# Column order of the one-pass matrix products in a fused Mamba-2 scan and low-rank mixer

## The chip, the cores and the metric

The kernel runs on one core of one Trainium2 chip. The metric is the device time of one execution in microseconds, from runs without the profiler; one more execution was recorded by the hardware profiler, and all times inside the kernel come from that one. Engines are named as the profile names them: PE is TensorE with PEld its weight loads, DVE is VectorE, ACT is ScalarE, POOL is GpSimd, SP is SyncE with its DMA queue SPq.

## The reference

A Mamba-2 scan over 4 batches, 8 heads, 768 positions, in chunks of 32, gives `x` of shape (4, 768, 256). A mixer follows, and its last two products are where this change lies:

```python
xt = x.transpose(0, 2, 1)
h = xt @ U @ V                            # U 768 x 32, V 32 x 768
u = x + h.transpose(0, 2, 1)
ch = np.maximum(u @ w_ch1, 0.0) @ w_ch2   # 256 -> 1024 -> 256
return (u + ch).astype(np.float32)
```

## The kernel before

**Layout.** The mixer works on `u` turned over: its 256 channels lie on the partitions (two halves, `NCB` = 2) and the tokens along the free dimension. The 768 tokens of a batch are cut into three blocks of 256 (`HS`). So there are twelve blocks, and a product is always 128 x 128 weights against 256 columns, one column for each token. `w_ch1` gives 1024 hidden channels, eight groups of 128 (`m`), of which a step takes two. The result of a step is a PSUM tile of 128 x 2 x 256, one bank; the banks carry the tags `x` and `z` (three each, by turns) and `w` (two).

**Two kinds of products.** The first two blocks of batch 0 are multiplied in full precision (`plain`, and the second branch of `down`): each such product shows as two MATMUL records. The other ten blocks use the type fp32r, of which a product shows as one record, a one-pass product. To keep precision, each fp32r operand is split into three tensors: a near part (`v` = 0), a far part (`v` = 1) and a combination of both (`v` = 2). The products of `v` = 0 and 1 are added up in PSUM, ACT scales the sum in place (`scaled`, L858), and the products of `v` = 2 are added on top.

**The steps.** For block `j` and step `i`, `first` (letter `f` in the plan) makes the products of `v` = 0 and 1, eight of them, and the scaling. `second` (`e`) adds the four of `v` = 2 and has ACT write the ReLU. `third` (`h`) makes the far and the combined tensors of the hidden channels on DVE. `down` (`d`) multiplies the hidden channels with `w_ch2`: for each `v`, each half `n` of the output channels and each half of the hidden groups a call of `products` with four of them, 48 in a block; after the last, DVE adds `u` and the block goes out. The very last block of batch 3 goes through `rows` instead, which has the hidden channels as weights and `w_ch2` as the 256 columns.

**How many.** Ten blocks have 16 products in `first` for each of `v` = 0 and 1, and 16 in `second`: 480. Nine blocks go through the one-pass branch of `down`, with 16 for each `v`: 432. `rows` has 48. That makes 960 one-pass products.

**What sets the order.** Nothing is scheduled by a tool: the long strings in `PLANS` name every step in the order in which it is written, and each engine runs its instructions in that order. The steps of the scan for batches 1 to 3 (`gram` L591, `inter` L721, `intra` L746, `state` L626) stand between the mixer's steps of earlier batches. From about 161 us on the scan is over and PE has products of the mixer alone.

**All products pass one line.** `nc.tensor.matmul` in `products` (L853) issues them all; its tiles tell them apart: `x<-u,w` and `z<-u,w` are `first` and `second`, `x<-words,w` and `z<-words,w` are `down`, `x<-w,words` and `z<-w,words` are `rows`, and those with `yT,w1f` or `words,o` the full-precision ones. Operands are dense: the 256 columns of `rhs` and of the PSUM half lie side by side in a partition. A few products elsewhere are not dense: `keep` (L394, L397) writes PSUM in groups of 8 columns with gaps of 8 between them, and `gram` (L591) reads its 128 columns alternately from two places that lie 128 elements apart.

Of the kernel before, what the change touches and what calls it, by code (L numbers as in the profile page):

```python
# [74 lines left out]
def kernel(  # L75
# [27 lines left out]
    nc = tc.nc  # L103
# [46 lines left out]
    def bank(tag, *dims):  # L150
        t = psum.tile([P, *dims], FP32, tag=tag, name=tag, bufs=BANKS[tag])
        if any(fills):
            flat = t if len(dims) == 1 else t.rearrange(
                {2: "p a b -> p (a b)", 3: "p a b c -> p (a b c)"}[len(dims)])
            small(flat, fills[1])
            idle(flat, fills[0])
        fills[:] = 0, 0
        return t
# [7 lines left out]
    class Kept:  # L166
# [23 lines left out]
        out=a_sb,  # L190
# [4 lines left out]
    pairs = [(b, q) for b in range(NB) for q in range(NPR)]  # L195
# [122 lines left out]
    for v in range(2):  # L318
        half = slice(v * H, v * H + H)
# [15 lines left out]
    for g in range(2):  # L335
# [3 lines left out]
        out=la.rearrange("p b c h -> p b h c"),  # L339
# [19 lines left out]
    for v in range(2):  # L359
        half = slice(v * H, v * H + H)  # L360
# [110 lines left out]
    def prep(k, c=0, n=2):  # L471

        b, q = pairs[k]
        if "BC" not in st.setdefault(k, {}):
            st[k]["BC"] = att.tile([P, 2, 2, NH, N], FP32, tag="BC", name="BC")
        for g in [slice(4) if n == 2 else slice(c, c + 1) if c < 2 else slice(2, 4)]:
            part = st[k]["BC"].rearrange("p i c h n -> p (i c) h n")[:, g]
            vector.tensor_tensor(
                out=part, in0=bc_sb[k].rearrange("p h i c n -> p (i c) h n")[:, g],
                in1=F[:, b, q].rearrange("p h i c -> p (i c) h")[:, g, :, None].to_broadcast(  # L480
                    part.shape), op=ALU.mult)
# [316 lines left out]
    def mixer(b):  # L798
# [35 lines left out]
        def block(j):  # L834
            return uT[:, :, ts(j, HS)]
# [12 lines left out]
            vector.tensor_tensor(out=far, in0=u, in1=near.bitcast(FP32), op=ALU.subtract)  # L848
            joined(near, far, both)

        def products(t, pairs, start):
            for lhsT, rhs in pairs:
                nc.tensor.matmul(out=t, lhsT=lhsT, rhs=rhs, start=start, stop=True,  # L853
                                 skip_group_check=True)
                start = False

        def scaled(t):
            nc.scalar.activation(t, t, AF.Copy, scale=1.0 + EPS)  # L858

        def words(dtype):  # L860
            t = raw.tile([P, 2 * WCOLS], INT32, tag="words", name="words", bufs=NWORDS)
            return t.bitcast(dtype).rearrange("p (v m t) -> p v m t", v=2, m=2)

        def plain(j, i):

            if i % 2 == 0:
                gT[j, i // 2] = words(FP32)
            t = bank("xz"[i % 2], 2, HS)
            for m in range(2):
                products(t[:, m], [(w1f[i][:, n, ts(m, P)], block(j)[:, n]) for n in range(NCB)],  # L870
                         m == 0)
            nc.scalar.activation(gT[j, i // 2][:, i % 2], t, AF.Relu)

        def terms(j, m, which):
            return [(w1[v][:, n, ts(m, P)], us[j][v][:, n]) for v in which for n in range(NCB)]

        def first(j, i):

            gs["t", j, i] = t = bank("xz"[i % 2], 2, HS)
            for m in range(2):  # L880
                products(t[:, m], terms(j, 2 * i + m, (0, 1)), m == 0)
            scaled(t)

        def second(j, i):

            t = gs["t", j, i]
            for m in range(2):
                products(t[:, m], terms(j, 2 * i + m, (2,)), False)
            if i % 2 == 0:
                gs["both", j, i // 2] = words(FP32R)  # L890
            nf = words(FP32R)
            gs[j, i] = [nf[:, 0], nf[:, 1], gs["both", j, i // 2][:, i % 2]]
            nc.scalar.activation(gs[j, i][0], t, AF.Relu, scale=NEAR)  # L893
# [43 lines left out]
        def down(j):  # L937

            def terms(n, which, half):
                return [(w2[v][:, m, ts(n, P)], gs[j, m // 2][v][:, m % 2])  # L940
                        for v in which for m in range(NQ * half, NQ * half + NQ)]

            def added_to(t, n=slice(None), sl=slice(None)):
                u = block(j)[:, n, sl]
                vector.tensor_tensor(out=u, in0=t[:, n, sl], in1=u, op=ALU.add)

            t = bank("xz"[j % 2], NCB, HS)
            if b or j >= PLAIN:
                for v in range(3):
                    for n in range(NCB):  # L950
                        for half in range(2):
                            products(t[:, n], terms(n, (v,), half), v + n + half == 0)
                            if v == 1 and n and half:
                                scaled(t)
                            if v == 2 and n and half:
                                added_to(t)
                            yield
            else:
                for n in range(NCB):
                    for half in range(2):  # L960
                        products(t[:, n], [(w2f[m // 2][:, m % 2, ts(n, P)],
                                            gT[j, m // 4][:, m // 2 % 2, m % 2])
                                           for m in range(NQ * half, NQ * half + NQ)],
                                 n + half == 0)
                        if n and half:
                            added_to(t)
                        yield
            if b or j == NBL - 1:
                o = mix.tile([P, 2 * WCOLS], FP32, tag="o", name="o") if b else raw.tile(
                    [P, 2 * WCOLS], FP32, tag="words", name="words", bufs=NWORDS)  # L970
                o = o[:, :NCB * HS].rearrange("p (n i) -> p n i", n=NCB)
                vector.transpose(out=o, in_=block(j))
                for r in range(4):
                    nc.sync.dma_start(
                        out=out[b, ts(j, HS)].rearrange(
                            "(k t) (n a c) -> a t n k c", t=Q, n=NCB, c=Q)[r],
                        in_=o[ts(r, Q)].rearrange("p n (k c) -> p n k c", c=Q))
                yield
                return
            o = raw.tile([P, 2 * WCOLS], FP32, tag="words", name="words", bufs=NWORDS)  # L980
            o = o[:, :HS // P * DM].rearrange("p (k n d) -> p k n d", k=HS // P, n=NCB)
            t = bank("w", HS // P, NCB, P)
            for n in range(NCB):
                for k in range(HS // P):
                    nc.tensor.transpose(out=t[:, k, n], in_=block(j)[:, n, ts(k, P)],
                                        identity=ident)
            nc.scalar.copy(out=o, in_=t)
            nc.sync.dma_start(
                out=out[b].rearrange("(j k p) m -> j p k m", j=NBL, p=P)[j],
                in_=o.rearrange("p k n d -> p k (n d)"))  # L990
            yield
# [4 lines left out]
        def piece(j):  # L996
            next(downs.setdefault(j, (rows if b >= ROWS and j == NBL - 1 else down)(j)))

        return SimpleNamespace(p=project, x=mixed, a=added, S=split, f=first, e=second, h=third,
                               d=piece, U=plain)  # L1000

# [10 lines left out]
    def spread():  # L1012

        nc.scalar.copy(out=UU, in_=U_sb[:, :, None].to_broadcast([P, NC, 2, RK]))

        v = [bank(t, VS // 2) for t in "xz"]
        for q in range(4):
            for i in range(2):
                nc.tensor.matmul(out=v[i][ts(q, Q)],
                                 lhsT=ident.rearrange("p (r q) -> p q r", q=4)[:, 2 * (q % 2) + i],  # L1020
                                 rhs=Vq, start=True, stop=True, skip_group_check=True)
        for i in range(2):
            nc.scalar.copy(out=V4[:, ts(i, VS // 2)], in_=v[i])
# [32 lines left out]
    def ytokens_of(k, v):  # L1056
# [6 lines left out]
                 j=crossed, y=yout, t=sided, L=load, Q=lambda k, c: prep(k, c, 1),  # L1063
# [4 lines left out]
                 v=lambda n: spread())  # L1068
# [54 lines left out]
```

## Time and profile before

| | us |
|---|---|
| three runs | 214.03, 215.01, 215.75 |
| median | 215.01 |
| span of the profiled execution, first to last instruction | 216.2 |
| last MATMUL starts in the profiled execution | 212.8 |

The profiled execution has no time of its own beside its span. The span is 1.2 us above the median of the runs and 0.4 us above the longest. A sum made from its rows is therefore used as a difference, and put on the median. "Busy" of PE joins overlapping matmuls; the pace of a row of products is better read from start to start, which the timeline gives: a row there is a run of equal instructions with the start of the first, the time to the end of the last, and their count.

### The profile page before, as it was taken

The numbers are of one execution on the slowest core, as the hardware profiler recorded it, in microseconds if no ns is written. First come the engines' busy times: TensorE is split into PE (matmuls) and PEld (weight loads), VectorE is DVE, ScalarE is ACT, GpSimd is POOL, SyncE is SP. The second block draws the span as 40 slices with busy tenths as digits, with TensorE's granted clock in tenths as the row PEclk, the third lists the DMA queues.
The fourth block names the chain that finished last, engine by engine and source line by source line (L and its number), as shares of the span: only waits on it lengthen the run. The fifth ranks groups of instructions, "written<-read, shape, count | busy, mean of one in ns | idle before, by whom it ended". The sixth has DMA issues, their size and how long they took to land.

```text
span 216.2 us, 7556 instructions
## 1 busy us (share of the span) xinstructions
PE 205.8 (95%) x3214; PEld 183.6 (85%) x3214; DVE 173.4 (80%) x363; ACT 121.0 (56%) x279; POOL 6.3 (3%) x22
## 2 busy tenths in 40 slices
PE   7988987999999999999999999899999999999994
PEld 4766755787889997998999998589998999999993
DVE  4498869988999999999899986759966398759841
ACT  3454646659968857186488451668612675444310
POOL 4121000000000000000000000000000000000000
PEclk9999997999999999999999999999999999999999
DMA  6998677996553379447666846544600000323344
GB/s 89 123 117 197 76 186 170 218 247 149 77 71 52 65 195 124 110 60 102 92 103 108 190 91 150 80 74 100 137 12 0 0 5 0 52 38 64 48 97 97
DMA packets 120177, 21.43 MB, mean 99 GB/s; under 512 B 110096, under 2 KB 118352, under 8 KB 120144
## 3 DMA queue, kind: packets, MB, share of 16 engines
q1 hardware_dynamic: 120144, 20.95, 53.3%
q8 instruction: 25, 0.41, 0.9%
q14 instruction: 8, 0.07, 0.1%
HBM read 14.39 MB, written 6.55 MB: 97 GB/s over the span
## 4 chain that ended last, share of the span: by engine, by line
PE 62%; DVE 22%; SPq 5%; ACT 4%; issue 3%; DMA 2%; POOL 0%; DVEq 0%; POOLq 0%; ACTq 0%
PE x L853 28%; PE z L853 21%; DVE words L177 7%; SPq L203 5%; DVE S L177 3%; DMA words<-in_moe_w_ch_dram 2%; DVE yT L177 2%; DVE w L177 2%; DVE M L177 2%; DVE BC L177 1%; PE x L139 1%; PE w L626 1%; PE x L591 1%; DVE u L177 1%; PE z L746 1%
## 5 line engine op out<-in xcount | busy, mean ns | idle before, releaser
L177 DVE SCALAR_TENSOR_TENSOR words<-words 128x512 fp32r<-128x512 f32 (+6 forms) x60 | 39.3, 668 | 2.6 <-ACT words L429 0.5
L853 PE MATMUL x<-words,w 128*128 128x256 f32 x288 | 38.5, 281 | 0.1
L853 PEld LDWEIGHTS x<-words,w 128*128 128x128 f32 x288 | 35.3, 189 | 1.8 <-issue 1.2
L853 PE MATMUL x<-u,w 128*128 128x256 f32 x240 | 34.6, 283 | 0.0
L853 PE MATMUL z<-u,w 128*128 128x256 f32 x240 | 33.0, 279 | 0.0
L858 ACT ACTIVATE x<-x 128x512 f32<-128x512 f32 (+1 forms) x27 | 15.5, 577 | 29.6 <-PE x L853 27.5
L853 PEld LDWEIGHTS x<-u,w 128*128 128x128 f32 x240 | 30.5, 188 | 0.6 <-ACT yT L766 0.3
L853 PEld LDWEIGHTS z<-u,w 128*128 128x128 f32 x240 | 30.0, 188 | 0.1
L858 ACT ACTIVATE z<-z 128x512 f32<-128x512 f32 (+1 forms) x24 | 13.6, 572 | 12.7 <-PE z L853 12.7
L853 PE MATMUL z<-words,w 128*128 128x256 f32 x144 | 19.9, 282 | 0.0
L853 PEld LDWEIGHTS z<-words,w 128*128 128x128 f32 x144 | 18.1, 189 | 0.9 <-issue 0.9
L177 DVE SCALAR_TENSOR_TENSOR words<-x,words 128x512 fp32r<-128x512 f32 x20 | 13.7, 683 | 5.4 <-ACT words L893 5.4
L177 DVE SCALAR_TENSOR_TENSOR words<-z,words 128x512 fp32r<-128x512 f32 x20 | 13.6, 682 | 2.3 <-ACT words L893 2.2
L893 ACT ACTIVATE words<-x 128x512 fp32r<-128x512 f32 x20 | 12.0, 598 | 3.6 <-PE x L853 3.6
L591 PE MATMUL x<-Cm,T 32*64 32x128 f32 x192 | 12.1, 310 | 1.6 <-DVE yT L177 1.2
L177 DVE TENSOR_TENSOR yT<-x,yT 128x384 f32<-128x384 f32 (+1 forms) x15 | 9.2, 614 | 5.5 <-PE x L853 2.7
L177 DVE SCALAR_TENSOR_TENSOR S<-S,kept,w 128x64 f32<-128x64 f32 x40 | 11.2, 279 | 2.3 <-PE w L626 0.6
L893 ACT ACTIVATE words<-z 128x512 fp32r<-128x512 f32 x20 | 11.8, 598 | 1.9 <-PE x L853 1.3
L658 ACT ACTIVATE Sm<-S,slot 128x128 f32<-128x128 f32 (+1 forms) x18 | 6.0, 386 | 9.9 <-DVE S L177 9.9
L591 PEld LDWEIGHTS x<-Cm,T 32*64 32x64 f32 x192 | 7.5, 131 | 4.1 <-DVE yT L177 1.5
L177 DVE TENSOR_TENSOR BC<-bc,F 128x512 f32<-128x512 f32 (+2 forms) x18 | 8.8, 517 | 2.6 <-ACT F L379 1.3
L591 PE MATMUL z<-Cm,T 32*64 32x128 f32 x192 | 10.5, 311 | 0.0
(154 smaller groups left out, 368.5 us busy)
## 6 DMA issues: line engine op xcount, KB each, us to landing
words<-in_moe_w_ch_dram SPq DMA_DIRECT2D x7, 512.0 KB, 5.3
squares<-w1f SPq DMA_DIRECT2D x52, 64.0 KB, 1.9
x<-in_x_dram SPq DMA_DIRECT2D x24, 128.0 KB, 4.0
out_dram<-o SPq DMA_DIRECT2D x32, 64.0 KB, 2.2
bc<-in_B_dram SPq DMA_DIRECT2D x24, 64.0 KB, 3.5
bc<-in_C_dram SPq DMA_DIRECT2D x12, 128.0 KB, 3.8
T<-squares SPq DMA_DIRECT2D x6, 256.0 KB, 3.9
ytok<-squares SPq DMA_DIRECT2D x6, 256.0 KB, 3.1
```

Source lines behind the costliest of these rows:

```text
L139: nc.tensor.matmul(out=t[:, :m * w].rearrange("p (m i) -> p m i", i=w), lhsT=ident, rhs=ident[:, None, :w].to_broadcast([P, m, w]), start= ...
L177: self.last = call(*args, **kwargs)
L203: op = nc.sync.dma_start(**kwargs)
L591: nc.tensor.matmul(out=g[r][cols, c], lhsT=s["T"][rows, 0, c, cols], rhs=s["Cm"][rows, :, :, ts(2 * c + p, Q)].rearrange("r v t i -> r v i ...
L626: nc.tensor.matmul(out=s["A"][p][ts(r, Q), v], lhsT=s["bd"][half, v, 2 * r:2 * r + 2].rearrange("p h n -> p (h n)"), rhs=x_sb[k][half, v, ...
L658: nc.scalar.activation(s["Sm"][:, sl, v], s["S"][:, sl, ts(v, D)], AF.Copy, scale=slot[:, v, None])
L746: product = nc.tensor.matmul(out=y[n][p][ts(v, Q), c], lhsT=x_sb[k][half, c, h], rhs=s["M"][half, h // 2, c, h % 2], start=fresh(k, n, p, ...
L853: nc.tensor.matmul(out=t, lhsT=lhsT, rhs=rhs, start=start, stop=True, skip_group_check=True)
L858: nc.scalar.activation(t, t, AF.Copy, scale=1.0 + EPS)
L893: nc.scalar.activation(gs[j, i][0], t, AF.Relu, scale=NEAR)
```

## The change

`products` takes a width. Where one is given, the 256 columns of the PSUM half and of `rhs` are both walked in another sequence: they are cut into groups of `width` columns, the even groups are taken first and the odd ones after them. Each column still meets its own column of the result, so the sums are the same. The first products of a sum (`v` = 0), the full-precision ones and those of `rows` keep the plain order; `first` takes 64 for `v` = 1, `second` takes 16, and `down` takes 32 for `v` = 1 and 4 for `v` = 2.

```diff
+        def columns(t, width):
+
+            return t.rearrange("p (a b c) -> p b a c", b=2, c=width) if width else t
+
-        def products(t, pairs, start):
+        def products(t, pairs, start, width=None):
             for lhsT, rhs in pairs:
-                nc.tensor.matmul(out=t, lhsT=lhsT, rhs=rhs, start=start, stop=True,
-                                 skip_group_check=True)
+                nc.tensor.matmul(out=columns(t, width), lhsT=lhsT, rhs=columns(rhs, width), start=start,
+                                 stop=True, skip_group_check=True)
                 start = False
...
-                products(t[:, m], terms(j, 2 * i + m, (0, 1)), m == 0)
+                products(t[:, m], terms(j, 2 * i + m, (0,)), m == 0)
+                products(t[:, m], terms(j, 2 * i + m, (1,)), False, 64)
             scaled(t)
...
-                products(t[:, m], terms(j, 2 * i + m, (2,)), False)
+                products(t[:, m], terms(j, 2 * i + m, (2,)), False, 16)
...
-                            products(t[:, n], terms(n, (v,), half), v + n + half == 0)
+                            products(t[:, n], terms(n, (v,), half), v + n + half == 0,
+                                     (None, 32, 4)[v])
```

No instruction moves: on every engine the same ones stand in the same order with the same waits, and only the shape of the columns differs. On PE near the end of the kernel before, where the `e` step of one block and `down` of another alternate (`u_3087` is the combined tensor of a block of `u`, `w_79` that of `w_ch1`; `w_82` and `w_83` are the far and the combined tensors of `w_ch2`):

```order
L853 MATMUL x<-words,w_82 128x256 x4
L853 MATMUL z<-u_3085,w_77 128x256 x2
L853 MATMUL z<-u_3086,w_78 128x256 x2
L853 MATMUL x<-u_3087,w_79 128x256 x4
L853 MATMUL x<-words,w_83 128x256 x12
```

The same place now:

```order
L857 MATMUL x<-words,w_82 128x2x4x32 x4
L857 MATMUL z<-u_3085,w_77 128x256 x2
L857 MATMUL z<-u_3086,w_78 128x2x2x64 x2
L857 MATMUL x<-u_3087,w_79 128x2x8x16 x4
L857 MATMUL x<-words,w_83 128x2x32x4 x12
```

The last number of a shape is the width of a group, the one before it how many groups of one kind there are, and the 2 ahead of it stands for even and odd.

## The prediction

> **What bounds the kernel now.** I read the page first: how busy each engine is, the clock granted to PE, the chain that ended last, and the groups of L853.
>
> ```profile
> PE 205.8 (95%) x3214; PEld 183.6 (85%) x3214; DVE 173.4 (80%) x363; ACT 121.0 (56%) x279; POOL 6.3 (3%) x22
> PEclk9999997999999999999999999999999999999999
> PE 62%; DVE 22%; SPq 5%; ACT 4%; issue 3%; DMA 2%; POOL 0%; DVEq 0%; POOLq 0%; ACTq 0%
> L853 PE MATMUL x<-words,w 128*128 128x256 f32 x288 | 38.5, 281 | 0.1
> L853 PE MATMUL x<-u,w 128*128 128x256 f32 x240 | 34.6, 283 | 0.0
> L853 PE MATMUL z<-u,w 128*128 128x256 f32 x240 | 33.0, 279 | 0.0
> L853 PE MATMUL z<-words,w 128*128 128x256 f32 x144 | 19.9, 282 | 0.0
> ```
>
> The reader sees PE busy for 95% of the span, most of the chain on PE, and 912 one-pass products with 0.1 us of idle time ahead of them in all. Next I took the stages, with the time of each engine in a stretch, the granted clock and the DMA share.
>
> ```profile
> 69.00:100.00 31.00, 30.84 (x467) 27.63 (x474) 30.13 (x61) 20.22 (x45) 0.00 (x0) 1.00 0.58 106
> 100.00:127.00 27.00, 27.00 (x512) 25.71 (x506) 25.22 (x49) 16.95 (x42) 0.00 (x0) 1.00 0.66 119
> 127.00:161.00 34.00, 33.30 (x610) 30.22 (x610) 26.59 (x54) 18.21 (x46) 0.00 (x0) 1.00 0.48 94
> 161.00:213.00 52.00, 52.00 (x444) 51.03 (x440) 34.96 (x55) 22.47 (x42) 0.00 (x0) 1.00 0.21 35
> ```
>
> Columns: length, PE, PEld, DVE, ACT, POOL, clock, DMA share, GB/s. The one-pass products begin in the first of these stretches. From there on the clock is 1.00, and the last 52 us are PE from end to end, while DVE has a third of them free. So a nanosecond on a product there is a nanosecond on the kernel; before 161 us nearly so, since PE lacks only 0.9 us of 92 in the first three rows.
>
> What sets the pace of a product? Its mean duration (281) overlaps its neighbours; the pace is read from start to start in the timeline.
>
> ```profile
> 73.34 0.60 PE L985 MATMUL w<-ident,yT 128*128 128x128 f32 x4
> 73.78 3.62 PE L853 MATMUL z<-words,o 128*128 128x256 f32 x16
> ...
> 119.82 1.52 PE L853 MATMUL x<-words,w 128*128 128x256 f32 x12
> 121.18 0.62 PE L853 MATMUL z<-words,w 128*128 128x256 f32 x4
> ...
> 168.16 2.05 PE L853 MATMUL z<-u,w 128*128 128x256 f32 x16
> 170.05 0.64 PE L853 MATMUL x<-u,w 128*128 128x256 f32 x4
> ```
>
> Twelve one-pass products take 121.18 - 119.82 = 1.36 us, 113 ns each; sixteen later take 170.05 - 168.16 = 1.89 us, 118 ns each. Both paces hold for long stretches and don't go with a tile. Two neighbours are quicker for the same work. A full-precision record of 256 columns goes over them twice: with the 379 ns of one record taken off the 3.62 us, (3.62 - 0.38) / 15 = 216 ns, or 108 ns for 256 column steps. A transpose, which also loads 128 x 128 weights, goes at (0.60 - 0.27) / 3 = 110 ns, with one duration of 272 ns taken off; the rows of these two durations:
>
> ```profile
> L853 PE MATMUL z<-words,o 128*128 128x256 f32 x32 | 7.4, 379 | 0.0
> L985 PE MATMUL w<-ident,yT 128*128 128x128 f32 x8 | 1.2, 272 | 0.0
> ```
>
> So a one-pass product has 108 ns of columns, and 5 to 10 ns more from elsewhere. In that pair of operations a weight load of 128 columns stands against each 256 columns, and the last stage's row has PEld busy for 51.03 of 52 us. [...] Then columns may become 5 to 10 ns slower before anyone sees it.
>
> **The change part by part.** It adds no instruction, no wait and no transfer, and its order on each engine is unchanged; SP's and POOL's queues aren't touched. Of the 960 one-pass products 608 walk their columns in groups: 160 in groups of 64 (`first`), 160 of 16 (`second`), 144 of 32 and 144 of 4 (`down`). Of the 144 of width 4, five blocks' worth, 80, stand in the last 52 us. The only unknown is what a jump between groups costs, on the side of PSUM and on the side of the columns read.
>
> On the PSUM side the trace has a pair: `keep` writes 192 dense columns at L387, and 192 in groups of 8 with gaps of 8 at L394.
>
> ```profile
> 7.89 0.49 PE L387 MATMUL z<-la,after 128*128 128x192 f32 x2
> 8.22 0.43 PE L389 MATMUL z<-la,onward 128*128 128x160 f32 x2
> 8.49 0.49 PE L394 MATMUL z<-la,middle 128*128 128x192 f32 x2
> 8.82 0.43 PE L397 MATMUL z<-la,high 128*128 128x160 f32 x2
> 9.09 0.43 PE L397 MATMUL z<-la,low 128*128 128x160 f32 x2
> ```
>
> L387 takes 8.22 - 7.89 = 0.33 us and L394 8.82 - 8.49 = 0.33 us: gaps in PSUM cost nothing there. They are full-precision products, which go over their columns twice; whether one pass is as forgiving, no row shows. [...]
>
> On the reading side the nearest row is `gram`, whose neighbouring columns lie 128 elements apart, so that every column is a jump.
>
> ```profile
> 125.92 0.30 PE L591 MATMUL x<-Cm,T 32*64 32x128 f32 x2
> 125.93 0.30 PE L591 MATMUL z<-Cm,T 32*64 32x128 f32 x2
> 125.95 0.30 PE L591 MATMUL x<-Cm,T 32*64 32x128 f32 x2
> 125.96 0.30 PE L591 MATMUL z<-Cm,T 32*64 32x128 f32 x2
> 126.06 0.30 PE L591 MATMUL x<-Cm,T 32*64 32x128 f32 x2
> ...
> 126.20 0.30 PE L591 MATMUL x<-Cm,T 32*64 32x128 f32 x2
> ```
>
> Eight records, side by side on different parts of the array, start every 126.20 - 126.06 = 0.14 us. Each goes twice over 128 columns, 256 column steps: 140 ns against 108 for dense ones. Part of the 32 ns may be the array's four row strips and not the jumps. So the price for 256 scattered steps is 0 to 32 ns if each pass pays alone, and up to 64 if one pass has to fetch as many columns as two did there.
>
> Width 4 has 64 groups in 256 columns. I take the scattered price for it, 140 ns, as the nearest row that I have, though fewer jumps may cost less. In the last 52 us that is 80 x (140 - 118) = 1.8 us; for the other 64, at paces of 113 and 118, 64 x (140 - 115.5) = 1.6 us. Widths 16, 32 and 64 have 16, 8 and 4 groups. At the same price for a jump they add 32 x 16/64 = 8 ns, 4 and 2 to the 108, which ends at 116 or below: within 3 ns of the load's cover, at most 160 x 3 = 0.5 us at the pace of 113 and nothing at 118, so nothing is taken. If that cover is gone, by loads at the transposes' 110, they cost 160 x 6 + 144 x 2 = 1.2 us. DVE and ACT get later products and wait; in the last stage DVE's 35 of 52 us leave room. The sum is +3.4 us. Bounds for width 4 are 0 and 144 x (172 - 116) = 8.1 us.
>
> The profiled execution ran 216.2, 1.2 above the median 215.0; the difference goes on the median: 215.0 + 3.4 = 218.4.
>
> **The rivals.**
>
> *Nothing is seen.* Groups of 4 are as good as dense, or slower by less than the load covers. For it speak L394 and the 5 to 10 ns of cover. The time is 215.0, give or take what the two paces make: should the last stage fall to 113 ns, 440 x 5 = 2.2 us are gained, and the earlier stretches at 118 would lose as much. Chance 0.26.
>
> *Faster.* The 5 to 10 ns above 108 need not be the load's own: they may be the column reads and the weight reads getting in each other's way, with two ways of falling into step (113 and 118). Columns in another sequence would then break the step. At the transposes' 110, the 272 changed products of the last stage gain 8 ns each and the 336 before it about 5.5: 2.2 + 1.8 = 4.0 us, 211.0; the pace of 113 in the last stage alone would give 212.8. I name 212.0. For it: a transpose loads equally many weights and is 3 to 8 ns quicker. Against it: each pace holds through many tiles at different places. [...] Chance 0.22.
>
> *Much slower.* [...] Chance 0.07 and 0.05.
>
> **How the numbers follow.** The forecast, width 4 at the scattered price, has the rest: 0.40, with its own range 216.5 to 223. About 1%, 2.2 us, is what a measurement of this kernel can tell from no change. Faster by more than that: 0.21 of the faster rival and 0.03 of a lucky pace, 0.24. Within it: 0.22 of the rival without effect, 0.05 of a small price for width 4, 0.01 of a weak gain, 0.28. Slower: 0.35 of the forecast, 0.12 of the much slower rival and 0.01 of an unlucky pace, 0.48. The range runs from 211.0, the faster rival's full gain, to 223.0, the upper bound of width 4: beyond it lie 0.12 above and some 0.06 below.
>
> **What would show it.** In the changed kernel's timeline of the last stage, `down` with `w_83` (width 4) should go at about 140 ns from start to start, the rest at 113 to 118 as before, and PE should stay without gaps up to the last product, which starts some 3 us later. Width 4 at 118 or less shows the first rival; widths 64 to 4 at 110 or below the second; any width at 200 or above the third. The forecast is wrong if width 4 isn't the slowest of the four, or if plain-order products change their pace too: then the cause lies in the loads and not in the columns.

## The result, and the profile after

| | before | after |
|---|---|---|
| median of 13 runs each, us | 214.13 | 216.71 |
| lowest and highest | 213.32, 216.94 | 215.94, 220.88 |
| span of the profiled execution | 216.2 | 215.0 |

The changed kernel is slower: ratio 1.0125, 95% interval 1.0098 to 1.0153, which on 214.13 is 2.7 us (2.1 to 3.3). The ratio leaves out runs more than 1.5% above the fastest of their kernel, such as the one of 220.88. The profiled execution after took 216.69, at its median; so 1.7 us lie around its span. With as much around its span of 216.2, that of before took some 217.9, an estimate that is above each of its 13 runs, and its clock row has a slice of 7 that the other has not. The two spans can't be set against each other, but the stretch of one-pass products can, with care. It runs from the start of the first to that of the last: 69.5 to 212.8 before, 67.1 to 211.5 after, 143.3 and 144.4 us.

The page of the changed kernel, with the rows that answer to those of before:

```profile
PE 205.9 (96%) x3214; PEld 183.7 (85%) x3214; DVE 173.4 (81%) x363; ACT 121.0 (56%) x279; POOL 6.3 (3%) x22
...
PEclk9999999999999999999999999999999999999999
...
PE 82%; DVE 6%; SPq 4%; ACT 2%; DMA 2%; issue 2%; POOL 0%; DVEq 0%; POOLq 0%; ACTq 0%
...
L857 PE MATMUL x<-words,w 128*128 128x256 f32 x288 | 38.9, 282 | 0.1
...
L857 PE MATMUL x<-u,w 128*128 128x256 f32 x240 | 34.9, 285 | 0.0
L857 PE MATMUL z<-u,w 128*128 128x256 f32 x240 | 33.4, 281 | 0.0
...
L857 PE MATMUL z<-words,w 128*128 128x256 f32 x144 | 20.1, 283 | 0.0
```

Each group of products has grown by 0.2 to 0.4 us, and nothing else has appeared: no new wait, the same counts. Where it sits shows in the timeline near the end, where the kernel's order tells which products a row holds. Before, all in plain order (24 products, then the 16 of `down` with `v` = 2):

```profile
202.56 2.99 PE L853 MATMUL z<-words,w 128*128 128x256 f32 x24
205.38 1.10 PE L853 MATMUL x<-w,words 128*128 128x256 f32 x8
206.32 2.05 PE L853 MATMUL z<-words,w 128*128 128x256 f32 x16
208.21 1.11 PE L853 MATMUL x<-w,words 128*128 128x256 f32 x8
```

After, first eight products of `second` (groups of 16) and then the same two rows, now with 8 plain and 16 products in groups of 32, and with 16 in groups of 4:

```profile
194.67 0.65 PE L857 MATMUL x<-u,w 128*128 128x256 f32 x4
195.16 0.65 PE L857 MATMUL z<-u,w 128*128 128x256 f32 x4
195.64 1.11 PE L857 MATMUL x<-u,w 128*128 128x256 f32 x8
...
201.28 3.00 PE L857 MATMUL z<-words,w 128*128 128x256 f32 x24
204.12 1.10 PE L857 MATMUL x<-w,words 128*128 128x256 f32 x8
205.06 2.05 PE L857 MATMUL z<-words,w 128*128 128x256 f32 x16
206.95 1.10 PE L857 MATMUL x<-w,words 128*128 128x256 f32 x8
```

Groups of 16 take (195.64 - 194.67) / 8 = 121 ns. Groups of 4, for which 140 was forecast, take (206.95 - 205.06) / 16 = 118, exactly what plain order took at this place before. The same by all starts of the trace (from each product to the next at this line, pauses of over 135 ns left out, sorted by the shape of the first):

| kernel, products | count | mean ns |
|---|---|---|
| before, all | 921 | 116.2 |
| after, plain order | 343 | 116.0 |
| after, groups of 64 | 155 | 115.6 |
| after, groups of 32 | 134 | 119.7 |
| after, groups of 16 | 150 | 120.9 |
| after, groups of 4 | 141 | 117.9 |

So the price rises from 64 to 16 and falls again to 4. Against the 116.2 of before it sums to 160 x 4.7 + 144 x 3.5 + 144 x 1.7 - 160 x 0.6 = 1.4 us. This is near the 1.1 us that the stretch grew between the two profiles, but only half of the 2.7 us that the ratio gives.

### The profile page after: what moved, and what is told of

Same layout as the page of the kernel before. It is cut to its first block, busy times and chain, and to the rows that moved or that the text cites. A ratio compares the mean times of both kernels' runs of the same rounds, so it can differ in the third digit from the quotient of the medians.

```text
span 215.0 us, 7556 instructions
## 1 busy us (share of the span) xinstructions
PE 205.9 (96%) x3214; PEld 183.7 (85%) x3214; DVE 173.4 (81%) x363; ACT 121.0 (56%) x279; POOL 6.3 (3%) x22
## 4 chain that ended last, share of the span: by engine, by line
PE 82%; DVE 6%; SPq 4%; ACT 2%; DMA 2%; issue 2%; POOL 0%; DVEq 0%; POOLq 0%; ACTq 0%
PE x L857 37%; PE z L857 29%; SPq L203 4%; DMA words<-in_moe_w_ch_dram 2%; DVE words L177 2%; PE w L626 2%; PE z L746 2%; PE x L746 1%; PE x L591 1%; PE x L139 1%; PE w L810 1%; PE x L822 1%; PE x L721 1%; PE w L139 1%; ACT yT L766 1%
## 5 line engine op out<-in xcount | busy, mean ns | idle before, releaser
L591 PE MATMUL x<-Cm,T 32*64 32x128 f32 x192 | 11.5, 307 | 1.0 <-DVE yT L177 0.6
L177 DVE TENSOR_TENSOR M<-x,causal 128x256 int32<-128x256 int32 x24 | 9.0, 419 | 1.7 <-PE z L591 1.7
```

Source lines behind the costliest of these rows:

```text
L177: self.last = call(*args, **kwargs)
L591: nc.tensor.matmul(out=g[r][cols, c], lhsT=s["T"][rows, 0, c, cols], rhs=s["Cm"][rows, :, :, ts(2 * c + p, Q)].rearrange("r v t i -> r v i ...
```

## The experiments

### One width alone

Two theories. A: each width has a price of its own, and the others go as before. B: the grouped products knock the plain ones out of the quicker of the two paces, 113 ns. Beside the kernel before, once more, three kernels kept one width each (`...` stands for the unchanged arguments):

```diff
 # 16 alone
-                products(..., False, 64)
+                products(..., False, None)
-                                     (None, 32, 4)[v])
+                                     (None, None, None)[v])
 # 32 alone: 64 and 16 to None, and
+                                     (None, 32, None)[v])
 # 4 alone: 64 and 16 to None, and
+                                     (None, None, 4)[v])
```

> The kernel before, once more, for the spread of its two paces. Theory A (each width has a price of its own) needs the plain-order products at the same mix of 113 and 118 ns in both kernels, some 116 ns on the mean. Theory B (the changed widths knock the other products out of the 113 ns pace) expects this kernel to show mostly 113 ns in a run without a half-clock stretch, below 115 on the mean. Ratio 1.00.

> Only the 160 products of `second` keep their groups, of 16; all others in plain order. Theory A: these go at 121 ns from start to start as in the changed kernel, the rest as before: 160 x 5 = 0.8 us slower, ratio 1.004. Theory B: nearly the whole loss, 2 us or more, ratio 1.010, with plain-order products mostly at 118 ns.

> Only the 144 products of `down` with v = 1 keep their groups, of 32. Theory A: 119.7 ns each, 144 x 3.7 = 0.5 us slower, ratio 1.0025. Theory B: as with 16, ratio 1.010.

> Only the 144 products of `down` with v = 2 keep their groups, of 4. Theory A: 118.0 ns each, 144 x 2 = 0.3 us slower, ratio 1.0013. Theory B: ratio 1.010. The forecast's own term, 140 ns each and 3.4 us, has already fallen by the changed kernel's trace; if it came back here, ratio 1.016.

| kernel | ratio, 95% interval | grouped products, mean ns | plain ones, mean ns |
|---|---|---|---|
| before again | 0.9986 (0.9942 to 1.003) | | 116.4 |
| 16 alone | 1.004 (1.0008 to 1.0072) | 120.9 | 114.7 |
| 32 alone | 1.0098 (1.0056 to 1.0139) | 119.9 | 116.5 |
| 4 alone | 1.0052 (1.0011 to 1.0093) | 118.0 | 115.0 |

The prices of the widths come back to within 0.2 ns, so they belong to the grouped products themselves: theory A for the pace. In time, 16 alone costs about what A said (0.9 us, 0.2 to 1.5, against 0.8). 32 alone costs 2.1 us against 0.5, and the lower end of its interval, 1.2, is still above: more than A. 4 alone has an interval from 0.2 to 2.0 us with A's 0.3 in it. B as it was put, the whole loss for any width, falls with 16 alone. The time of 32 alone would fit B, but its plain products, at 116.5 ns, go as in the kernel before. 16 alone even had its last products, which are in plain order, at the quick pace: (208.83 - 207.02) / 16 = 113 ns, where before they took 118. Its timeline:

```profile
207.02 1.98 PE L857 MATMUL z<-w,words 128*128 128x256 f32 x16
208.83 1.07 PE L857 MATMUL x<-w,words 128*128 128x256 f32 x8
```

Which pace a stretch has is thus not fixed. The kernel before, run again, spreads from 213.06 to 217.29, and its profile, of the execution of 217.29, has 118 ns in the last stage.

What lies ahead of the one-pass products is the same in all these kernels, and yet it differs by more than the terms in question. From the starts of the products in the traces:

| kernel | first one-pass product, us | last one, us | between them | slower by its ratio |
|---|---|---|---|---|
| before | 69.5 | 212.8 | 143.3 | |
| before again | 68.5 | 212.1 | 143.7 | |
| the change | 67.1 | 211.5 | 144.4 | 2.7 |
| 16 alone | 67.8 | 210.5 | 142.7 | 0.9 |
| 32 alone | 69.1 | 213.0 | 143.9 | 2.1 |
| 4 alone | 68.0 | 210.6 | 142.6 | 1.1 |

In 32 alone the one-pass stretch is 0.2 to 0.6 us longer than in the two profiles before, which is A's price and no more. In 16 and 4 alone it is shorter than in both, since more of the plain products go at 113 ns, and still these kernels take longer. So the two profiles before don't show a usual execution of their kernel: they are of 217.29 us and some 217.9 us, where the medians are 215.14 and 214.13. Whether a usual one is shorter ahead of the one-pass products or in their pace, no trace shows.

### 16 everywhere, on both sides, on one side

Is the price the width's or the place's, and is it paid where columns are read or where results are written?

```diff
 # 16 everywhere
+                products(..., False, 16)
+                                     (None, 16, 16)[v])
 # the same, read side alone
-                nc.tensor.matmul(out=columns(t, width), lhsT=lhsT, rhs=columns(rhs, width), start=start,
+                nc.tensor.matmul(out=t, lhsT=lhsT, rhs=columns(rhs, width), start=start,
 # the same, result alone
+                nc.tensor.matmul(out=columns(t, width), lhsT=lhsT, rhs=rhs, start=start,
```

> All 608 products that the change touches take groups of 16, in `first`, `second` and `down` alike. If the price belongs to the width (theory A), all of them go at 121 ns, and the kernel is 608 x 5 = 3.0 us slower, ratio 1.014. If it belongs to the place (the weights or the tiles of `second`), only those of `second` do, and the products of `down` stay at 118 or less.

> As the last, but only the columns that are read go in groups of 16; the result is written in plain order, so that the output's columns are mixed up within a block. Reading-side theory: 121 ns as with both. PSUM-side theory: 113 to 118 ns as in plain order.

> Only the result is written in groups of 16, the columns are read in plain order; the output's columns are mixed up within a block. Reading-side theory: 113 to 118 ns. PSUM-side theory: 121 ns. If each side has half of the price, about 118 in both of these kernels.

The 16 products of `down` with `v` = 2 near the end, in the timelines of the three kernels in this order:

```profile
207.89 2.11 PE L857 MATMUL z<-words,w 128*128 128x256 f32 x16
209.84 1.10 PE L857 MATMUL x<-w,words 128*128 128x256 f32 x8
```

```profile
207.08 2.10 PE L857 MATMUL z<-words,w 128*128 128x256 f32 x16
209.02 1.11 PE L857 MATMUL x<-w,words 128*128 128x256 f32 x8
```

```profile
204.74 2.05 PE L857 MATMUL z<-words,w 128*128 128x256 f32 x16
206.62 1.11 PE L857 MATMUL x<-w,words 128*128 128x256 f32 x8
```

122, 121 and 118 ns; over all, 120.9, 120.8 and, for the result alone, 116.4 for all its products, as before. The plain products of the first two kernels took 117.3 ns, 1 ns more than before, so the grouped ones slow their neighbours a little too, or these had less of the quick pace. The ratios go along: 1.0214 (1.0103 to 1.0325), 1.0203 (1.0067 to 1.0339), and 0.9999 (0.9939 to 1.0058). The price is the width's, in `down` as in `second`, and all of it is paid on the reading side. Writing in groups of 16 is free (116.4 ns against 116.2), as at L394 for groups of 8 in full-precision products: its two records took 0.33 us, and so did the two in plain order at L387.

### Groups of 2

```diff
+                products(..., False, 2)
+                                     (None, 2, 2)[v])
```

> All 608 in groups of 2, shorter than in the change. A price for each jump (128 of them) above that of width 4 would show 125 ns or more; the forecast's scattered row gives 140 to 172 ns, 15 to 34 us more. If the price follows the distance between groups and not their number, it stays at 115 to 121 ns.

283.94 us, ratio 1.3241 (1.306 to 1.3422). The same 16 products, (273.65 - 269.99) / 16 = 229 ns each:

```profile
269.99 3.83 PE L857 MATMUL z<-words,w 128*128 128x256 f32 x16
273.65 1.12 PE L857 MATMUL x<-w,words 128*128 128x256 f32 x8
```

Here is the cliff, between 4 and 2, and it is a doubling: 229 against 118. No run shows its cause. An estimate from the 229 ns: a least time of 229 / 128 = 1.8 ns for each of the 128 groups would leave 115 for the 64 groups of width 4, below their 118. 608 x 112 ns is 68 us, and the kernel is 69 us slower, so what a product loses here arrives at the end in full.

To see which side pays here, and what a width between 4 and 16 costs, one kernel gave each set of products its own shape (the pair is the width of the result and of the columns read):

```diff
+                products(..., False, (8, 8))
+                products(..., False, (2, None))
+                                     ((None, None), (None, 2), (8, 8))[v])
```

> Each group of products has a shape of its own: `first` (v = 1) groups of 8 on both sides, `second` groups of 2 in the result alone, `down` (v = 1) groups of 2 in the columns read alone, `down` (v = 2) groups of 8 on both sides; columns are mixed up where one side alone is grouped. If only the reading side has a price: `second` 113 to 118 ns, `down` v = 1 at 228 as with groups of 2 on both sides, the kernel 144 x 112 = 16 us slower. If PSUM takes part in the price of 2: `second` well above 118. Width 8: 118 to 121.

The timeline, with the products of `second` (result in groups of 2), then 8 plain ones and 16 that read in groups of 2, and at last 16 in groups of 8:

```profile
208.96 0.62 PE L857 MATMUL z<-u,w 128*128 128x256 f32 x4
209.41 1.09 PE L857 MATMUL x<-u,w 128*128 128x256 f32 x8
...
215.04 4.78 PE L857 MATMUL z<-words,w 128*128 128x256 f32 x24
219.63 1.14 PE L857 MATMUL x<-w,words 128*128 128x256 f32 x8
220.60 2.08 PE L857 MATMUL z<-words,w 128*128 128x256 f32 x16
222.52 1.11 PE L857 MATMUL x<-w,words 128*128 128x256 f32 x8
```

Writing in groups of 2 takes (209.41 - 208.96) / 4 = 113 ns here, the quick pace, and 116.5 over all 150 starts, against 116.7 for the same products before: free as well. Reading in groups of 2 takes (4.59 us - 8 x 0.118) / 16 = 228 ns. Groups of 8 take 120 here and 118.3 over all 294: between 4 and 16, so the number of jumps doesn't order the widths. Ratio 1.078 (1.0658 to 1.0901), some 17 us where 16 was expected.

### Half the weight load

The prediction let the load of 128 weight columns cover slower reading, an assumption of its author. If the load sets 113 and 118 ns, half a load must quicken the products.

```diff
+                half = slice(H) if width else slice(P)
-                nc.tensor.matmul(out=columns(t, width), lhsT=lhsT, rhs=columns(rhs, width), start=start,
+                nc.tensor.matmul(out=columns(t[half], width), lhsT=lhsT[:, half],
+                                 rhs=columns(rhs, width), start=start,
```

> The widths of the change, but the 608 products in groups use only the first 64 of their 128 weight columns (half of the output's partitions miss these terms), so that each loads half as many weights; plain-order products keep 128. Theory S (reading in groups is itself slower than the weight load): 16 stays at 121 ns, 32 at 120, 4 at 118. Theory L (column reads and weight reads get in each other's way): with half the load all four widths go at 108 to 113 ns and differ by less than 2 ns.

> Again with 64 weight columns for the grouped products, but other widths: `first` 128, which is the plain order, `second` 8, `down` 16 and 32 (half of the output's partitions miss these terms). Theory S: plain order near 108, 16 at 121 and 32 at 120 in these places too. Theory L: all at 108 to 113 ns. Width 8 has 32 groups: by number of jumps it would be dearer than 16, by distance between 4 and 16.

The second kernel ran with other widths than its expectation names: 8 in `first`, 2 in `second`, 16 and 64 in `down`. Plain order with half a load, which its expectation speaks of, was not tried. The two took 216.80 and 237.92 us in one run each, which gives no interval. The weight loads of the first one by shape, and the products of `second` in groups of 16 in its timeline:

```profile
L858 PEld LDWEIGHTS z<-u,w 128*64 128x64 f32 x160 | 19.6, 135 | 0.1
L858 PEld LDWEIGHTS z<-u,w 128*128 128x128 f32 x80 | 12.2, 188 | 0.0
```

```profile
195.02 0.65 PE L858 MATMUL x<-u,w 128*64 128x256 f32 x4
195.50 0.64 PE L858 MATMUL z<-u,w 128*64 128x256 f32 x4
195.99 1.11 PE L858 MATMUL x<-u,w 128*128 128x256 f32 x8
```

A load is down from 188 to 135 ns, and the products still take (195.99 - 195.02) / 8 = 121 ns. Over all: 64 at 115.0 (115.6 with full loads), 32 at 117.9 (119.7), 16 at 120.4 (120.9), 4 at 117.1 (117.9). In the second kernel 16 took 120.4 in `down`, 8 took 117.7, 64 took 118.2 and 2 took 228. That is theory S for 16, 8 and 4, while 32 lost about half of its price. Weight reads in the way of column reads (theory L) would have brought all of them to 108 to 113 ns; halving the load took away 0.5 to 1.8 ns.

So the load doesn't hide the slower reading of 16 and 32. Nor do the products of this stretch of the trace before wait for the end of their loads' rows:

```profile
211.87 1.01 PEld L853 LDWEIGHTS z<-w,words 128*128 128x128 f32 x8
211.98 1.10 PE L853 MATMUL z<-w,words 128*128 128x256 f32 x8
```

The eight loads end at 212.88, while the last of their products starts at 212.8: a load's row ends some 0.07 us into its product. What sets 113 and 118 in plain order stays open. Half the weights shorten a load by 53 of 188 ns only, and a part of it that doesn't shrink isn't ruled out. Groups of 64, which cost nothing, went at 115.6 ns on the mean with full loads and at 115.0 and 118.2 in the two kernels with half.

### 32 everywhere

```diff
+                products(..., False, 32)
+                products(..., False, 32)
+                                     (None, 32, 32)[v])
```

> All 608 in groups of 32. If the pace of 119.9 ns that width 32 showed is all that it costs, 608 x 3.7 = 2.2 us, ratio 1.010. If the 2.1 us of the kernel with 32 alone (144 products) were its true price, 9 us, ratio 1.042.

Ratio 1.011 (1.0015 to 1.0204), and 119.6 ns over 581 products: the first reading. 608 products in groups of 32 cost 2.4 us (0.3 to 4.4) and 144 of them cost 2.1 us (1.2 to 3.0); at 1.2 us for 144, 608 would cost 5.1. The loss above the pace is therefore not a price for each product.

## Why the prediction was right, and where its steps were not

The time came out inside the forecast, 2.7 us slower against 3.4, with the sign and nearly the size. The size is luck: the one term of the sum was 3.2 us too large, two terms that were put at nothing make 1.25 us, and 1.3 us have no cause that a run shows. The sign follows from what did hold: reading in groups costs time, and a nanosecond on a product counts.

- **Bound.** That a nanosecond on a product counts in full held: groups of 2 cost 68 us on the products and 69 on the kernel.
- **Weight load as the cover.** That the load covers columns that are 5 to 10 ns slower was the author's assumption, and no run shows such a cover: half the load left 16 at 121 ns. So the price of width 16, put "within 3 ns of the load's cover", was not hidden (120.9 ns with full loads against 116.2 in plain order), and that of 32 wasn't either (119.7).
- **The 108 ns** were an estimate: a full-precision record of 256 columns took 216 ns, near twice the 113 and 118 ns of a one-pass product, and half of it was put for going over them once.
- **Width 4 at the scattered price.** 80 x 22 ns and 64 x 24.5 ns were forecast, 3.4 us; it is 144 x 1.7 = 0.24 us. `gram`'s row, in which every column is a jump, was the wrong neighbour: it goes at 140 ns, while groups of 4 take 118 and groups of 2 take 229, far above the prediction's highest figure of 172. Why `gram` is quicker than groups of 2 was not tried.
- **Widths 16, 32 and 64 at nothing.** 16 costs 160 x 4.7 = 0.75 us, 32 costs 144 x 3.5 = 0.5 us, 64 costs nothing. The ordering by number of jumps failed: width 4 is not the slowest of the four, which the prediction had named as a sign that it is wrong. It would then have put the cause into the loads; half a load shows that for 16 it isn't there (120.4 ns against 120.9).
- **The PSUM side at nothing** held, down to groups of 2 (116.5 ns against 116.7).
- **The rivals.** Faster needed the two reads to hinder each other; half a load took away 2 ns at most. Its broken step may be seen where plain products went at 115 ns on the mean in 16 and 4 alone, against 116.2 to 116.4 in the three traces that read in plain order throughout; but these three executions were longer than their medians, so it isn't shown. Much slower didn't come: no width of the change went above 121 ns on the mean, and twice the time exists on the reading side alone, at groups of 2 (228 ns).

The change's 2.7 us are thus shown in half: 1.4 us are the paces of 16, 32 and 4. The other 1.3 us (0.7 to 1.9 by the interval) stay open. In 32 alone as well 1.6 of 2.1 us lie outside the pace of its grouped products. What could hold them is the mix of 113 and 118 in plain-order products: the last stage of the kernel before at 113 ns would be 428 x 4.6 = 2.0 us quicker than the profiled one. The part ahead of the one-pass products could hold them as well: it took from 66.4 us (groups of 2) to 71.1 (the second kernel with half the load) over the traces, though it is the same in all. No trace of the kernel before near its median exists, so both are only argued.

## What to carry to other kernels

The 256 columns that such a one-pass product reads could be cut into groups of 4, 8, 16, 32 or 64 for 4% of the product's time at most (120.9 ns against 116.2); in groups of 2 the time doubled, and other widths were not tried. The order in which results are written to PSUM was free for groups of 16 and of 2 (116.4 and 116.5 ns). A term that "something else hides" should be tested by shrinking what hides it: here one term far too large covered for those that were put at nothing.

## What the runs showed of the hardware that was not expected

The price of the reading order is not monotone: 115.6 ns for groups of 64, 119.7 for 32, 120.9 for 16, 118.3 for 8, 117.9 for 4, 228 for 2. No run here shows why 16 and 32 are the worst above the cliff. One-pass products in plain order have two paces at a clock of 1.00, each of which holds over many tiles: in the kernel before 113.3 ns from 111 to 125 us, and 117.8 ns from 163 to 212 us. No run shows what sets them.
